# Which tile shape the products beside the weighings have, and a new list of pieces

## The chip, the cores and the metric

The kernel runs on one core of a Trainium2 chip. The metric is the device time of one execution in microseconds (us). Five engines work side by side, each through its own instructions in order: PE multiplies matrices (PEld is its loading of weights), DVE, ACT and POOL work element by element, SP issues most of the DMAs.

## The reference

What is computed, cut to what matters (S = 2048 rows, D = 512, 32 heads of width 16, 4 segments of L = 512 rows, F = 1792):

```
xn = layernorm(x)
q, k, v = xn @ wq, xn @ wk, xn @ wv           # split in heads and segments
for s in range(4):                            # M and z start at zero
    logits = q_s k_s^T * Dh**-0.5 + mask      # mask: -1e9 where the key lies after the query
    a_dot = softmax(logits) @ v_s
    a_mem = (phi(q_s) @ M) / (phi(q_s) @ z + 1e-6)
    o_s = g * a_mem + (1 - g) * a_dot         # g = sigmoid(beta), phi(t) = t + 1 if t > 0 else exp(t)
    M, z = M + phi(k_s)^T v_s, z + sum(phi(k_s))
out = x + o @ wo + silu(xn @ w1) @ w2
```

## The kernel before

The kernel is written as small pieces of work, and a list, ORDER, says in which order they are issued. Each word of the list is a piece's name followed by its numbers; the loop at L765 calls the functions of the table PIECES one after the other. Nothing is rearranged afterwards: every engine meets its own instructions in the order of the list, and semaphores make it wait for the others. So the list is the schedule of all engines at once.

The work is cut by segment s (512 rows), by block dt of 128 columns (8 heads) and by tile of 128 rows (t over all 16, or j within a segment). The pieces that matter here:

- S (scores, L634), 80 of them: a fifth of the scores of one block of one segment. Its matmuls use a quarter of PE's rows each (16 or 32 rows, four at a time), and write the four banks of psS, of which there is one buffer. ACT takes the exponential of all 2048 columns (L650) into one of seven buffers Pb, and POOL sets what lies behind the diagonal to zero (L658). A new line of the list begins at each S.
- E and O (weigh, L668), 16 each: the weights Pb times the values V, for the even and the odd heads of a block. Its matmuls use a quarter of PE's columns each (32 of 128), four at a time. Ev, Ea, Ov, Oa copy the result (oraw, odd), and SP moves the sums of the weights into zraw (L692) and the odd heads' rows into oraw (L711).
- k, q, v and h: products of the normed rows with wk, wq, wv and w1; a product of 512 columns is cut into parts (dense, L319, dense_mm, L309). ha is the tanh of h (L439), hv finishes silu into hT (L444); kv, qv, vv (and ka, qa, va on ACT) copy the others.
- o (out_mm, L577): one of the 18 products that add up to an output tile: 14 with w2 (from hT) and 4 with wo (from oT). oh is the same for one half of the last tile's columns. st and sh add x and store (L570, L614). In the last segment the tiles 2 and 3 are summed in psS.
- m, t, f and g pieces: the memory M and the maps phi; n (L548): phi(q) times M; s (L450): phi(q) times z, in column tiles of 32; r, w and, in the last segment, R, W: reciprocals of the sums and their weighting; z and d (spread, L518): DMAs that spread them over the rows, two for each; zv, dv, nv: the products and the sum that make oT (L536, L546, L557).
- xs, xq, xi, xg: statistics of the layernorm; Nv: its norm (L293); X, Xa, Xv and XD: its transposes; busy: matmuls of zeros.

The four banks that are not psS are shared by all other results of PE (bank, L298, four buffers). All matmuls but those of S, E, O and s are whole: 128 rows by 128 columns, one weight load each.

Of the kernel before, what the change touches and what calls it, by code (L numbers as in the profile page):

```python
# [15 lines left out]
ORDER = """  # L16
ones0 ones1 zeros xs0 xs1 xq0 xi0 busy44 xq1 Nv0 xi1 X0.1 Nv1 Xa0.1 busy6 X1.1 Xa1.1 v0.0.0 v0.0.1 xs2 xs3 xq2 v0.0.2 v0.0.3 xq3 xi2 va0.0 v0.1.0 v0.1.1 Nv2 v0.1.2 v0.1.3 va0.1 xi3 X2.1 Nv3 odd tb Xv2.1 k0.0.0 k0.0.1 X3.1 Xv3.1 k0.1.0 k0.2.0 k0.1.1 k0.0.2 k0.0.3 kv0.0 q0.0.0 q0.0.1 q0.0.2 q0.0.3 qa0.0 k0.1.2 xs7 fa0.0 k0.1.3 k0.2.1
S0 kv0.1 k0.3.0 k0.2.2 xs4 xs6 xs5 k0.3.1 q0.1.0 q0.1.1 q0.1.2 q0.1.3 xg4.4 k0.3.2 qa0.1 q0.3.0
S2 k0.3.3 v0.3.0 k0.2.3 kv0.2 q0.3.1 v0.3.1 q0.3.2 fp0.2 v0.3.2 q0.3.3 v0.3.3 fa0.2 kv0.3
S1 v0.2.0 h0.10.0 h0.10.1 qv0.3 h0.10.2 h0.11.0 v0.2.1 h0.10.3 Nv5 h0.11.1 h0.11.2 Nv6 ha0.10 fp0.0 vv0.3  # L20
S6 Nv7 hv0.10 q0.2.0 v0.2.2 q0.2.1 Nv4 v0.2.3 h0.11.3 XD5 h0.1.0 h0.1.1 ha0.11 XD7 h0.1.2
S5 q0.2.2 xs10 q0.2.3 vv0.2 h0.1.3 h0.5.0 h0.5.1 ha0.1 hv0.11 XD6 h0.13.0 qv0.2 h0.5.2 h0.5.3 h0.7.0
S3 ha0.5 h0.13.1 fv0.2 XD4 h0.7.1 xs13 h0.13.2 h0.13.3 hv0.1 xs9 h0.7.2 h0.7.3 ha0.13 E0 Ev0
S7 k1.1.0 t0.2 hv0.5 k1.1.1 ha0.7 k1.1.2 k1.1.3 xs11 q1.1.0 fp0.3 q1.1.1 q1.1.2 hv0.13 kv1.1 hv0.7 q1.1.3
S9 v1.1.0 xs8 qv1.1 v1.1.1 k1.0.0 lw0 xg8.4 k1.0.1 k1.0.2 E1 Ev1
S4 v1.3.0 k1.0.3 v1.1.2 fa0.3 kv1.0 v1.3.1 v1.3.2 v1.1.3 h0.4.0 h0.4.1 vv1.1 Nv10 h0.4.2
S10 k1.2.0 k1.2.1 k1.2.2 v1.3.3 h0.4.3 h0.2.0 h0.2.1 fv0.3 Nv8 vv1.3 ha0.4 k1.2.3 h0.2.2
S8 fp0.1 hv0.4 h0.2.3 O0 ha0.2 h0.8.0 h0.8.1 h0.8.2 Ov0
S14 q1.3.0 q1.3.1 tanh kv1.2 q1.3.2 h0.8.3 hv0.2 v1.2.0 Nv11 h1.11.0 v1.2.1 t0.3 ha0.8 h1.11.1 Nv9 xs12 q1.3.3
S11 hv0.8 XD10 v1.2.2 h1.11.2 h1.11.3 XD8 v1.2.3 XD9 O1 ha1.11  # L30
S12 qv1.3 vv1.2 k1.3.0 Ov1 h0.6.0 k1.3.1 k1.3.2 xs15 h0.6.1 fv0.0 h0.6.2 h0.6.3 q1.0.0 ha0.6 q1.0.1 hv1.11
S17 q1.0.2 k1.3.3 fa0.1 h0.0.0 h0.0.1 hv0.6 v1.0.0 xs14 h0.0.2 XD11 kv1.3 h0.0.3 q1.0.3
S16 m0.2 qv1.0 mv0.2 v1.0.1 E2 v1.0.2 h0.3.0 ha0.0 Ev2
S13 q1.2.0 h0.3.1 hv0.0 q1.2.1 xg12.4 h0.3.2 v1.0.3 h0.9.0 q1.2.2 h0.3.3 t0.0 ha0.3 vv1.0 h0.9.1
S15 h0.12.0 q1.2.3 h0.12.1 h0.12.2 fv0.1 h0.9.2 hv0.3 h0.9.3 h1.9.0 kind h1.9.1 ha0.9 h1.9.2 qv1.2 hv0.9
S18 fp1.0 h0.12.3 O2 E3 t0.1 h1.9.3 fp1.1 ha0.12 ha1.9
S19 Ev3 Ov2 hv1.9 k2.2.0 hv0.12 k2.2.1 fa1.0 kv2.2 h1.0.0 h1.0.1 h1.0.2 m0.0 h1.0.3
S21 Nv15 h1.8.0 mv0.0 v2.1.0 O3 ha1.0 h1.8.1 h1.8.2
S22 h1.8.3 Ov3 v2.1.1 hv1.0 ha1.8 vv2.1 v2.2.0 v2.2.1 o0.0.9 h1.10.0 Nv13
# [12 lines left out]
S38 v2.0.0 v2.0.1 q2.2.0 h1.6.3 XD14 ha1.6 q2.2.1 hv1.3
S33 h1.12.0 vv2.0 h1.13.0 fv1.3 hv1.6 qv2.2 h1.12.1 h1.13.1 h1.13.2 h1.13.3 gp1.2 ha1.13 E6 XD12
S34 h1.12.2 h1.12.3 ha1.12 hv1.13 v2.3.0 Ev6 v2.3.1 vv2.3 q2.0.0 o0.3.8
S37 o0.3.17 gv1.2 o0.3.16 fp2.0 q2.0.1 o0.3.3 q3.3.0 qv2.0 o0.3.4 ga1.3 t1.3 o0.3.13
S35 O6 hv1.12 q3.3.1 Ov6 k3.1.0 k3.1.1 fa2.0
S39 o0.3.9 kv3.1 gv1.3 h1.2.0 qv3.3 o0.3.14 h1.2.1 h1.2.2 fp2.3 h1.2.3 E7 ha1.2 fv2.0 fp2.1
S47 q3.1.0 o0.3.2 q3.1.1 ga2.2 Ev7 o0.3.10 O7
S41 qv3.1 o0.3.6 Ov7 m1.2 o0.3.5 o0.3.7 o0.3.15 mv1.2 fa2.1 m1.0 o0.3.11 hv1.2
S45 s1 q3.0.0 o0.3.12 fv2.1 gp2.2 mv1.0 sv1 r1.0 fa2.3 q3.0.1 v3.0.0  # L60
S42 h2.3.0 qv3.0 r1.1 v3.0.1 h2.3.1 ha2.3 vv3.0 t2.0 o0.3.0 o0.3.1 xl1.0 st0.3 h1.7.0
S44 h2.4.0 h2.4.1 r1.2 v3.3.0 r1.3 v3.3.1 ha2.4 w1 h1.7.1
S40 hv2.3 o1.0.3 vv3.3 o1.0.6 h1.7.2 hv2.4 o1.0.9 gv2.2 ga2.0 z1.2 fv2.3 v3.1.0 h1.7.3 v3.1.1
S46 ha1.7 vv3.1 v3.2.0 z1.1 d1.2 o1.0.1 v3.2.1 d1.1 o1.0.5 zv1.2 E8
S43 vv3.2 h2.8.0 hv1.7 d1.0 o1.0.11 h2.8.1 Ev8 k3.2.0 ha2.8 q3.2.0 dv1.2 d1.3
S49 q3.2.1 zv1.1 hv2.8 qv3.2 k3.2.1 gp2.0 z1.3 ka3.2 O8 xl2.0 E9 dv1.1
S48 o1.0.4 o1.0.2 k3.0.0 o1.0.13 Ev9 Ov8 n1.1 k3.0.1 o1.0.7 nv1.1 ka3.0
S51 n1.2 nv1.2 o1.0.10 dv1.3 h2.0.0 dv1.0 o1.0.12 zv1.3 xl1.2 o1.2.4 h2.0.1 ha2.0 o1.2.5
S50 o1.0.8 n1.3 o1.2.16 o1.2.10 hv2.0 o1.2.8 o1.0.15 O9 z1.0
S57 gv2.0 nv1.3 o1.2.13 h2.2.0 gp2.1 o1.0.17 o1.2.9 xl1.1 fp2.2 h2.2.1 ha2.2 Ov9 o1.1.12 o1.2.17  # L70
S52 o1.1.10 o1.2.0 o1.2.1 hv2.2 zv1.0 o1.1.4 o1.1.3 o1.2.3 o1.2.12 ga2.3 n1.0 o1.0.0 nv1.0 o1.1.8
S54 o1.2.11 o1.1.9 fa2.2 o1.1.5 o1.0.14 o1.1.16 o1.2.6 mw1.0 E10
S53 o1.0.16 o1.2.15 Ev10 o1.2.7 h2.7.0 h2.7.1 ha2.7 o1.2.2 o1.2.14
S59 fv2.2 st1.0 h2.1.0 st1.2 h2.1.1 o1.1.11 ha2.1 gp2.3 hv2.1 o1.1.14 o1.1.17 hv2.7 h2.11.0
S55 o1.1.2 o1.1.13 h2.11.1 o1.1.0 o1.1.1 o1.1.15 ha2.11 t2.3 o1.3.6 o1.1.6
S56 O10 gv2.3 o1.3.17 mw1.2 t2.1 o1.3.2 ga2.1 xl1.3 o1.1.7 o1.3.3 t2.2 Ov10 hv2.11 o1.3.5 o1.3.11 st1.1
S58 h2.6.0 h2.6.1 ha2.6 m2.0 E11 mv2.0
S63 h2.5.0 o1.3.16 h2.5.1 Ev11 o1.3.14 ha2.5 O11 hv2.6 Ov11
S60 h2.13.0 mw2.0 o1.3.0 hv2.5 gp3.1 h2.13.1 h2.10.0 ha2.13 gv2.1 o1.3.7 h2.10.1 ha2.10 o1.3.1 hv2.13
S61 s2 o1.3.9 o1.3.15 h3.1.0 hv2.10 o1.3.13 h3.1.1 xl2.3 o1.3.4 sv2 ha3.1 r2.3 r2.2 r2.0  # L80
S62 k3.3.0 r2.1 ga3.3 o1.3.8 w2 k3.3.1 d2.1 o1.3.12 d2.3 fill o1.3.10 gp3.3 st1.3 hv3.1 h2.9.0
S64 h2.9.1 m2.2 kv3.3 h3.3.0 h3.3.1 o2.3.2 z2.3 mv2.2 ha2.9
S66 ha3.3 E12 o2.3.3 o2.3.8 hv2.9 h3.0.0 Ev12 h3.0.1 ha3.0
S67 o2.3.11 z2.1 gv3.3 h2.12.0 o2.3.5 o2.3.10 h2.12.1 dv2.3 hv3.0 hv3.3 h3.4.0 o2.3.4 o2.0.6 ha2.12 z2.0 dv2.1
S65 zv2.3 o2.3.6 o2.3.0 h3.4.1 hv2.12 o2.0.12 o2.3.9 z2.2 o2.0.8 d2.0 o2.0.9 o2.3.13 zv2.1 n2.3 gp3.2 d2.2 ha3.4
S69 o2.0.5 xl2.1 hv3.4 o2.0.11 nv2.3 o2.3.1 o2.0.3 n2.1 nv2.1 ga3.2 o2.3.12 E13 Ev13
S68 O12 o2.0.1 o2.2.9 o2.3.15 zv2.0 dv2.0 o2.2.10 o2.2.0 Oa12 o2.2.12
# [14 lines left out]
def kernel(  # L102
# [474 lines left out]
    def out_mm(s, j, i, half=None):  # L577
# [21 lines left out]
        if s == LAST and j >= 2:  # L599
            for other, out in fin_out:  # L600
                if other != key:
                    tc.declare_no_dep(mm.ins, out.ins, reason="the outputs lie in banks of their own")
# [196 lines left out]
```

## Time and profile before

| | |
|---|---|
| median of 3 runs | 230.03 us (230.0 to 230.35) |
| the profiled execution | 231.8 us |
| its span, first to last instruction | 230.2 us |
| PE, ACT, DVE, POOL busy | 219.2, 199.3, 174.1, 113.3 us |
| exponentials (L650) | 80, 1.88 us each |
| instructions in the span | 5197 |

A row of the profile names the line of the kernel, the engine, the operation, what is written and read (out<-in), its shape and how often it ran; behind the bar stand the busy time and the mean of one in ns, then the idle time of the engine just before and what ended it. A timeline's row begins with the start and the length in us of one instruction, or of several merged (x4). For a matmul 16*128 or 32*128 are row tiles, 128*32 are column tiles and 128*128 is whole. Matmuls overlap: one of 512 columns shows as 0.38 us, and the next starts 0.216 us after it. "issue" stands for time in which an engine waited for nothing that the profile shows.

### The profile page before, as it was taken

How to read it: one execution, taken by the hardware profiler on the slowest of the kernel's cores; microseconds unless marked ns; L12 is line 12 of the kernel's file. 1: busy time of each engine (PE TensorE's matmuls, PEld its weight loads, DVE VectorE, ACT ScalarE, POOL GpSimd, SP SyncE). 2: the span in 40 equal slices, each digit the busy share in tenths (PEclk: the TensorE clock that was granted, in tenths of full speed). 3: DMA queues.
4: the chain of work that ended last, by engine and by line, in shares of the span. 5: the costliest groups of instructions: out<-in, count | busy, mean ns of one | idle time of the engine just before them, and what ended most of it. 6: DMA issues, size and time to landing. Idle time of an engine off the chain costs nothing.

```text
span 230.2 us, 5197 instructions
## 1 busy us (share of the span) xinstructions
PE 219.2 (95%) x1952; PEld 103.9 (45%) x1984; DVE 174.1 (76%) x348; ACT 199.3 (87%) x182; POOL 113.3 (49%) x173
## 2 busy tenths in 40 slices
PE   8999999999999999999999999999999999999993
PEld 8766544455434334343433433334343343435441
DVE  4789999997799587777698775585887765974833
ACT  3799999999999999999999999999999999893000
POOL 6049477656654576654944466353475355422000
PEclk9999999999999999999999999999999999999998
DMA  6993355132104532221023212161132211133122
GB/s 175 371 381 79 50 150 196 39 73 55 30 23 95 159 87 85 61 47 32 10 77 90 70 42 78 49 95 37 38 93 80 61 40 57 53 92 88 29 86 93
DMA packets 34777, 20.40 MB, mean 89 GB/s; under 512 B 15680, under 2 KB 34240, under 8 KB 34752
## 3 DMA queue, kind: packets, MB, share of 16 engines
q1 hardware_dynamic: 32128, 17.45, 27.4%
q10 hardware_dynamic: 2624, 2.62, 3.7%
q8 instruction: 15, 0.25, 0.5%
q14 instruction: 10, 0.08, 0.1%
HBM read 9.96 MB, written 2.10 MB: 52 GB/s over the span
## 4 chain that ended last, share of the span: by engine, by line
PE 69%; DVE 9%; ACT 8%; issue 5%; SPq 2%; POOL 2%; DMA 2%; DVEq 0%; ACTq 0%
PE ps L315 24%; PE psO L596 21%; PE psS L643 9%; PE psV L677 7%; ACT Pb L650 6%; PE ps L326 3%; ACT th L439 2%; PE psS L737 2%; DVE xn_t L293 2%; SPq L524 1%; PE psM L401 1%; DVE hT L444 1%; DVE stats L270 1%; POOL Pb L658 1%; DMA spr<-rz 1%
## 5 line engine op out<-in xcount | busy, mean ns | idle before, releaser
L650 ACT ACTIVATE Pb<-psS 128x2048 bf16<-128x2048 f32 x80 | 150.2, 1878 | 4.3 <-PE psS L643 3.2
L658 POOL TENSOR_SCALAR_AFFINE_SELECT Pb<-Pb 128x512 bf16<-128x512 bf16 (+1 forms) x112 | 80.5, 732 | 85.1 <-ACT Pb L650 84.9
L596 PE MATMUL psO<-w_sb,hT 128*128 128x512 bf16 x186 | 59.1, 381 | 0.8 <-issue 0.6
L444 DVE SCALAR_TENSOR_TENSOR hT<-th,ps 128x512 bf16<-128x512 bf16 x56 | 37.7, 681 | 16.1 <-ACT th L439 15.7
L315 PE MATMUL ps<-xnT,w_sb 128*128 128x512 bf16 x159 | 47.1, 380 | 0.8 <-issue 0.6
L596 PEld LDWEIGHTS <-hT 128*128 128x128 bf16 x238 | 21.8, 98 | 25.1 <-issue 6.2
L439 ACT ACTIVATE th<-ps 128x512 bf16<-128x512 f32 x56 | 32.7, 597 | 0.4 <-PE ps L315 0.4
L315 PEld LDWEIGHTS <-w_sb 128*128 128x128 bf16 x168 | 15.2, 98 | 18.3 <-issue 3.8
L677 PE MATMUL psV<-Pb,Vz 128*32 128x128 bf16 (+3 forms) x512 | 22.4, 302 | 0.5 <-DVE Vz L358 0.3
L596 PE MATMUL psO<-wo_sb,oT 128*128 128x512 bf16 x53 | 18.8, 380 | 0.3 <-issue 0.2
L643 PE MATMUL psS<-qT,kT 16*128 16x512 bf16 (+3 forms) x256 | 17.3, 302 | 0.9 <-ACT Pb L650 0.4
L315 PE MATMUL ps<-wv_sb,xnT 128*128 128x512 bf16 x60 | 18.1, 380 | 0.1
L643 PE MATMUL psS<-qT,kTo 32*128 32x512 bf16 (+3 forms) x256 | 17.2, 300 | 0.7 <-ACT Pb L650 0.4
L677 PEld LDWEIGHTS <-Vz 128*32 128x32 bf16 x512 | 11.0, 96 | 14.3 <-issue 4.6
L326 PE MATMUL ps<-xnT,w_sb 128*128 128x256 bf16 x112 | 16.4, 273 | 0.2 <-DVE z L414 0.2
L342 POOL TENSOR_SCALAR kTo<-kT,pm_odd 128x512 bf16<-128x512 bf16 x16 | 11.7, 736 | 8.5 <-DVE kT L341 7.6
L315 PE MATMUL ps<-xnT,wq_sb 128*128 128x512 bf16 x46 | 14.3, 381 | 0.0
L315 PE MATMUL ps<-xnT,wk_sb 128*128 128x512 bf16 x44 | 13.6, 380 | 0.7 <-DVE oraw L700 0.5
L707 DVE CAST odd<-psV 128x512 bf16<-128x512 f32 x14 | 9.6, 687 | 5.4 <-PE psV L677 5.3
L643 PEld LDWEIGHTS <-kT 16*128 16x128 bf16 x256 | 5.8, 92 | 17.1 <-issue 16.6
L326 PEld LDWEIGHTS <-w_sb 128*128 128x128 bf16 x112 | 10.5, 98 | 4.9 <-issue 1.5
L700 DVE CAST oraw<-psV 128x512 bf16<-128x512 f32 x15 | 10.3, 687 | 3.0 <-PE psV L677 2.8
(96 smaller groups left out, 262.9 us busy)
## 6 DMA issues: line engine op xcount, KB each, us to landing
spr<-rz SPq DMA_DIRECT2D x56, 64.0 KB
x_res<-in_A_x_dram SPq DMA_DIRECT2D x16, 128.0 KB
out_dram<-o_out SPq DMA_DIRECT2D x15, 128.0 KB
w_sb<-in_B_w_dram SPq DMA_DIRECT2D x1, 1792.0 KB
w_sb<-in_B_w_dram ACTq DMA_DIRECT2D x1, 1792.0 KB
x_hi<-in_A_x_dram SPq DMA_DIRECT2D x2, 512.0 KB
oraw<-odd SPq DMA_DIRECT2D x64, 16.0 KB
wv_sb<-in_A_wv_dram SPq DMA_DIRECT2D x2, 256.0 KB
```

The lines of the kernel that those rows point to most:

```text
L315: nc.tensor.matmul(sts[s][key][:, :], lhsT=lhsT(ki), rhs=rhs(ki), start=(ki == 0), stop=(ki == DT - 1))
L326: nc.tensor.matmul(sts[s][name, i][:, cols], lhsT=w_sb[:, ki, i * P : (i + 1) * P], rhs=xnT[:, ki, cols], start=(ki == 0), stop=(ki == DT ...
L342: nc.gpsimd.tensor_scalar(out=kTo[:, dt, :], in0=kT[:, dt, :], scalar1=pm_odd[:, 0:1], scalar2=1.0, op0=ALU.mult, op1=ALU.mult,)
L439: nc.scalar.activation(out=th[:], in_=sts[s]["h", ft][:, :], func=AF.Tanh, scale=0.5)
L444: nc.vector.scalar_tensor_tensor(out=st["hT"][:, ft, :], in0=st.pop(("th", ft))[:], scalar=1.0, in1=st.pop(("h", ft))[:, :], op0=ALU.add, ...
L596: mm = nc.tensor.matmul(st["psO", *key], lhsT=lhsT, rhs=rhs, start=len(done) == 1, stop=len(done) == FT + DT)
L643: nc.tensor.matmul(psS[:, g, c0 : c0 + nq], lhsT=kk[rows, dt, kt * P : (kt + 1) * P], rhs=st["qT"][rows, dt, kt * P : L], start=True, stop ...
L650: exp = nc.scalar.activation(out=Pb[:, :, :], in_=psS[:, :, :], func=AF.Exp, scale=SCALE)
L658: mask = nc.gpsimd.affine_select(out=blocks, in_=blocks, compare_op=ALU.is_ge, fill=0.0, base=0, pattern=[[0, blocks.shape[1]], [1, P]], c ...
L677: nc.tensor.matmul(psV[32 * g : 32 * g + 32, kt * P : L], lhsT=Vzs[s % 2][:, kt, 4 * dt + g, par : par + 2, :].rearrange("p a d -> p (a d) ...
L700: copy(out=oraw[:], in_=sts[s].pop(("psV", 0))[:, :])
L707: copy(out=odd[:], in_=sts[s].pop(("psV", 1))[:, :])
```

## The change

1. A helper, product, writes a whole product either as before or as four matmuls of 32 columns of the weights each, at the four column tiles. All products call it (dense_mm, dense, m_mm, n_mm, out_mm). A pass over the list sets which form each has: behind an S the products take the form of the next E, O or s if it comes ahead of the next S, and are whole otherwise; behind an E, O or s they stay column tiles up to the next S.
2. out_mm can make a part of the columns: oc is a half, od a quarter. 28 products o are made as two halves each and 14 as four quarters.
3. The statistics of a norm can be issued in two pieces, xc (sums) and xd (variance), and the list does so for the first tiles.
4. The list is new from its first line to its last.

```diff
+    narrow = [False]
+    def product(out, lhsT, rhs, start, stop):
+        if not narrow[0]:
+            return [nc.tensor.matmul(out, lhsT=lhsT, rhs=rhs, start=start, stop=stop, skip_group_check=True)]
+        return [
+            nc.tensor.matmul(
+                out[c : c + 32], lhsT=lhsT[:, c : c + 32], rhs=rhs, start=start, stop=stop,
+                tile_position=(0, c), skip_group_check=True,
+            )
+            for c in range(0, P, 32)
+        ]
...
-    def out_mm(s, j, i, half=None):
+    def out_mm(s, j, i, half=None, part=0, parts=1):
...
+        here = slice(part * width // parts, (part + 1) * width // parts)
+        cols = slice(first + here.start, first + here.stop)
...
-        mm = nc.tensor.matmul(
-            st["psO", *key], lhsT=lhsT, rhs=rhs, start=len(done) == 1, stop=len(done) == FT + DT
-        )
+        mms = product(st["psO", *key][:, here], lhsT, rhs, len(done) == 4, len(done) == 4 * (FT + DT))
...
-    for word in ORDER.split():
-        piece = word.rstrip("0123456789.")
+    words = ORDER.split()
+    pieces = [word.rstrip("0123456789.") for word in words]
+    TILED = {"S": "rows", "E": "cols", "O": "cols", "s": "cols", "X": "whole", "busy": "whole"}
+    ahead = ["rows"] * (len(words) + 1)
+    for i in reversed(range(len(words))):
+        ahead[i] = TILED.get(pieces[i], ahead[i + 1])
+    now = "whole"
+    for i, (word, piece) in enumerate(zip(words, pieces)):
+        if piece in TILED:
+            now = TILED[piece]
+        elif piece in ("k", "q", "v", "h", "m", "n", "o", "oc", "od", "oh"):
+            now = ahead[i] if now == "rows" else now
+            now = "whole" if now == "rows" else now
+        narrow[0] = now == "cols"
         PIECES[piece](*(int(n) for n in word[len(piece) :].split(".") if n))
```

The list before the first scores, one stretch from the middle of each, and its end from the last three S on, before (-) and after (+):

```diff
-ones0 ones1 zeros xs0 xs1 xq0 xi0 busy44 xq1 Nv0 xi1 X0.1 Nv1 Xa0.1 busy6 X1.1 Xa1.1 v0.0.0 v0.0.1 xs2 xs3 xq2 v0.0.2 v0.0.3 xq3 xi2 va0.0 v0.1.0 v0.1.1 Nv2 v0.1.2 v0.1.3 va0.1 xi3 X2.1 Nv3 odd tb Xv2.1 k0.0.0 k0.0.1 X3.1 Xv3.1 k0.1.0 k0.2.0 k0.1.1 k0.0.2 k0.0.3 kv0.0 q0.0.0 q0.0.1 q0.0.2 q0.0.3 qa0.0 k0.1.2 xs7 fa0.0 k0.1.3 k0.2.1
+ones0 ones1 zeros xc0 xd0 xc1 xq0 xi0 Nv0 busy44 xd1 xq1 xc2 xi1 X0.1 Nv1 xd2 Xa0.1 busy6 v0.0.0 v0.0.1 xq2 X1.1 Xa1.1 xs3 v0.0.2 v0.0.3 xq3 v0.1.0 xi2 v0.1.1 v0.1.2 v0.1.3 odd Nv2 xi3 X2.1 va0.0 k0.2.0 va0.1 Nv3 Xv2.1 X3.1 Xv3.1 k0.0.0 k0.0.1 k0.0.2 k0.0.3 q0.0.0 kv0.0 tb q0.0.1 q0.0.2 xs4 q0.0.3 qa0.0 k0.2.1 q0.3.0 fa0.0 q0.1.0
...
-S56 O10 gv2.3 o1.3.17 mw1.2 t2.1 o1.3.2 ga2.1 xl1.3 o1.1.7 o1.3.3 t2.2 Ov10 hv2.11 o1.3.5 o1.3.11 st1.1
+S58 Ov10 gp3.3 E11 oc1.3.1.0 gv2.1 m2.0 o1.3.13 Ev11 h2.6.1 ha2.6 o1.3.11 mv2.0
...
-S78 r3.2 o2.1.17 o2.1.1 o2.1.4 r3.1 o2.1.8 r3.3 h3.13.1 w3 o2.1.0 xl3.1 o2.1.2 R0.3 ha3.7 hv3.6 o2.1.9 R0.2 ha3.13 hv3.7 o2.1.16 hv3.13 R0.1
-S75 o2.1.5 h3.11.0 h3.11.1 ha3.11 R0.0 o3.1.8 d3.0 h3.9.0 h3.9.1 o2.1.14 W0 ha3.9 o2.1.7
-S76 o3.1.12 o2.1.11 d3.2 d3.1 o2.1.10 hv3.11 o2.1.13 dv3.2 o2.1.6 h3.10.0 dv3.0 z3.1 o2.1.15 h3.10.1 ha3.10 oh2.0 oh1.0 oh8.0 o3.2.4 o3.2.1 o3.1.4 hv3.9 oh3.1 oh5.1 z3.0 st2.1 O15 z3.2 hv3.10 E15 dv3.1 o3.0.5 o3.1.10 oh5.0 o3.2.0 o3.2.11 Ea15 Oa15 oh11.0 oh13.1 zv3.0 o3.0.12 n3.0 oh12.0 n3.2 o3.0.13 oh9.0 o3.1.0 o3.1.13 o3.2.5 oh13.0 zv3.1 nv3.0 oh10.0 zv3.2 nv3.2 o3.1.7 o3.0.0 o3.2.13 R1.0 oh6.0 oh0.0 xl3.0 R1.1 R1.2 o3.2.14 o3.2.16 o3.0.4 o3.2.9 R1.3 n3.1 o3.2.3 o3.2.12 oh3.0 d3.3 oh4.1 o3.1.11 o3.0.11 oh16.1 nv3.1 o3.0.7 o3.0.8 o3.1.16 o3.0.6 oh1.1 oh15.1 o3.0.10 oh7.1 oh0.1 o3.1.1 o3.2.6 o3.0.9 o3.2.8 o3.2.15 W1 o3.1.2 oh4.0 oh15.0 o3.1.3 o3.1.5 dv3.3 oh7.0 o3.0.15 o3.0.14 n3.3 z3.3 oh16.0 o3.0.1 o3.2.2 oh10.1 o3.2.7 xl3.2 zv3.3 o3.2.10 oh14.0 nv3.3 o3.0.3 oh14.1 o3.2.17 o3.0.17 st3.2 o3.0.2 oh11.1 o3.0.16 oh12.1 oh17.1 st3.0 oh17.0 oh6.1 oh9.1 sh0 oh8.1 oh2.1 o3.1.9 o3.1.14 sh1 o3.1.17 o3.1.6 o3.1.15 st3.1
+S76 o2.1.8 d3.0 d3.1 h3.9.1 o2.1.9 oc2.1.10.1 h3.13.0 ha3.9 od2.1.12.0 oc2.1.11.1 h3.13.1 xl3.3 hv3.9 o3.0.12 o2.1.16 ha3.13 o2.1.13
+S75 o3.0.5 hv3.13 o2.1.4 o3.0.4 R0.2 W0 o2.1.17 z3.0 h3.10.0 o3.1.8 h3.10.1 dv3.0 z3.2 ha3.10 od2.1.12.1 st2.1 o3.0.0 o3.1.6
+S78 o3.0.9 hv3.10 dv3.1 o3.1.1 h3.11.0 o3.0.8 h3.11.1 dv3.2 E15 oh13.1 oh4.1 ha3.11 z3.1 o3.2.13 Ea15 oh12.1 hv3.11 oh6.1 oh10.1 o3.2.1 O15 Oa15 oh11.1 oh2.1 oh12.0 o3.0.1 zv3.0 oh13.0 n3.1 od3.1.11.3 oh3.1 zv3.1 o3.2.0 oh10.0 n3.0 o3.1.2 nv3.0 o3.0.7 nv3.1 o3.1.12 oh9.1 oh8.0 o3.2.5 oh11.0 o3.1.7 o3.2.6 o3.0.13 oh8.1 R1.1 R1.0 o3.2.9 o3.1.14 d3.3 R1.3 o3.2.14 oc3.0.3.0 oh0.0 o3.0.6 o3.2.8 oc3.0.11.1 zv3.2 o3.1.10 n3.2 o3.2.10 oh9.0 R1.2 oh1.1 oh15.0 W1 nv3.2 oh15.1 o3.2.4 oc3.0.11.0 o3.1.5 o3.0.14 o3.2.11 oh1.0 o3.2.12 o3.2.2 oh6.0 o3.2.16 oh2.0 z3.3 oh7.0 oh0.1 dv3.3 oh3.0 od3.0.10.0 oh14.0 od3.1.11.1 oc3.1.0.0 o3.0.15 zv3.3 od3.1.11.0 oc3.0.3.1 n3.3 oc3.1.9.0 oh4.0 o3.2.3 xl3.0 o3.1.16 nv3.3 o3.2.15 od3.0.10.1 od3.0.10.2 o3.2.7 oh5.0 oh16.0 oh16.1 od3.0.10.3 oh14.1 o3.2.17 oh17.0 oh17.1 o3.0.2 o3.0.16 o3.0.17 od3.1.11.2 xl3.1 st3.2 oc3.1.9.1 oh7.1 oh5.1 sh0 o3.1.17 sh1 oc3.1.0.1 o3.1.3 o3.1.15 o3.1.13 st3.0 o3.1.4 st3.1
```

## The prediction

> **What bounds the kernel now.** I read the page's busy shares and its chain first, then the busy times by stage, then the timelines of ACT and PE, then PE's groups kept apart by shape, and last the end of the run.
>
> ```profile
> PE 219.2 (95%) x1952; PEld 103.9 (45%) x1984; DVE 174.1 (76%) x348; ACT 199.3 (87%) x182; POOL 113.3 (49%) x173
> PE 69%; DVE 9%; ACT 8%; issue 5%; SPq 2%; POOL 2%; DMA 2%; DVEq 0%; ACTq 0%
> ```
>
> PE is busy 95% of the span and carries 69% of the chain. The three stages (before the first exponential starts, from there to the start of the last one, the rest) show ACT beside it:
>
> ```profile
> 13.02:205.76 192.74, 187.50 (x1717) 83.65 (x1744) 153.27 (x300) 188.39 (x164) 107.96 (x155) 1.00 0.29 77
> 205.76:230.20 24.44, 19.86 (x131) 10.15 (x132) 12.79 (x26) 3.55 (x4) 1.22 (x2) 0.97 0.25 76
> ```
>
> (Stage, length, then busy PE, PEld, DVE, ACT, POOL.) For 192.74 us PE (187.50) and ACT (188.39) are both full; in the last 24.44 us ACT is done and PE works alone. ACT's timeline in the middle shows the beat:
>
> ```profile
> 126.15 1.88 ACT L650 ACTIVATE Pb<-psS 128x2048 bf16<-128x2048 f32 x1
> 127.92 0.59 ACT L439 ACTIVATE th<-ps 128x512 bf16<-128x512 f32 x1
> 128.53 1.88 ACT L650 ACTIVATE Pb<-psS 128x2048 bf16<-128x2048 f32 x1
> ```
>
> An exponential starts every 2.38 us: 1.88 of its own, and a small ACT piece while PE makes the next scores in the one buffer psS. Between two scores PE has 2.38 us to fill with products. PE's timeline shows what a change of array shape costs:
>
> ```profile
> 128.85 0.59 PE L315 MATMUL ps<-xnT,wk_sb 128*128 128x512 bf16 x2
> 129.38 1.27 PE L677 MATMUL psV<-Pb,Vz 128*32 128x512 bf16 x32
> 130.58 0.39 PE L643 MATMUL psS<-qT,kTo 32*128 32x512 bf16 x4
> ```
>
> Two whole products of 512 columns start 0.21 apart (0.59 less 0.38 of one), so the second starts at 129.06. The weighings (tiles 32 wide) follow at 129.38, 0.32 later: 0.10 more. They stream 2560 columns, four tiles at a time; at 0.216 per 512 that is 1.08, and the scores come after 1.20: again 0.10 and a little. A change of shape costs about 0.10 us.
>
> **The change, part by part.** *Shapes.* I counted them along both lists. Before, PE changes shape 194 times: 80 scores (row tiles), 32 weighings and 3 sums (column tiles), all else whole. After it, every product of a stretch between two scores that holds a weighing or a sum is written as four column tiles, so the stretch has one change at each end: 160 in all. 34 fewer at 0.10 is 3.4 us of PE. The columns streamed are the same (464,640); 56 halves and 56 quarters stand for 42 whole products, 70 pieces more at some 2.5 ns (a 128-column product takes 56 ns, four take 223 against 216): 0.2 us.
>
> *The price of a narrow product.* 367 products become 1468 matmuls with 1468 weight loads; PE's program grows from 3970 to 6312 instructions. The weighings are the same form:
>
> ```profile
> L677 PE MATMUL psV<-Pb,Vz 128*32 128x512 bf16 x128 | 12.8, 388 | 0.5 <-DVE Vz L358 0.3
> L677 PE MATMUL psV<-Pb,Vz 128*32 128x256 bf16 x128 | 9.1, 273 | 0.0
> L677 PE MATMUL psV<-Pb,Vz 128*32 128x128 bf16 x128 | 7.3, 219 | 0.0
> L401 PE MATMUL psM<-Vz,phiK 128*128 128x128 bf16 x48 | 3.7, 220 | 0.2 <-issue 0.2
> L596 PEld LDWEIGHTS <-hT 128*128 128x128 bf16 x238 | 21.8, 98 | 25.1 <-issue 6.2 <-DVE hT L444 0.3
> L677 PEld LDWEIGHTS <-Vz 128*32 128x32 bf16 x512 | 11.0, 96 | 14.3 <-issue 4.6 <-DVE hT L444 2.6 <-DVE oT L557 0.8
> ```
>
> One of 128 columns takes 219 ns narrow and 220 whole, and 32 matmuls in the 1.20 us above run at the pace of their columns. So I take 0 extra. From the other side: what the trace shows is short runs, at most 64 instructions in 1.20 us, 18.8 ns each; if lasting streams went no faster, eight would take 150 ns, which leaves 512-column products alone and adds 41 ns to a half and 94 to a quarter. In the other direction nothing is to be gained, since the columns are the same. The Trainium skill speaks against the change here: "TensorEngine Tiling (Array Packing)", in its restrictions, says that column tiling turns the fast weight load off. By that rule alone four loads in a row, at the row's 96 ns, would make a product 384 ns and the run some 82 us longer. The trace differs: 512 loads of 32 columns keep PEld busy for 11.0 us, 86 ns for four, so they overlap; I keep 0.
>
> *The stretches.* For each stretch I added its columns (0.216 per 512), its changes (0.10) and took the longest of PE's sum, the beat of 2.38, and 2.73 where ACT has two small pieces (the spacing of exponentials in such stretches). The 79 stretches give 192.57 before, against 192.74 in the trace. After, PE streams 2.75 us more in them (171.39 for 168.65) with 32 fewer changes, and the same sum gives 192.63: +0.06. So the middle doesn't get shorter: the freed time is filled with products taken from the end (2.1 us) and from ahead of the first scores (0.4).
>
> *The end.* PE's work after the last scores falls from 19.88 us to 17.54 (streaming 19.48 to 17.34; changes 4 to 2). Before, the last scores start at 205.31 and PE's last product at 226.14: 20.83, where the sum has 19.66, so 1.17 were waits. They belong to a chain through DMAs (chain of waits, then PE's timeline):
>
> ```profile
> 213.56 0.50 SPq L692
> 214.11 1.54 DMA zraw<-odd
> 215.67 1.78 DVE ri L507 x4
> ...
> 222.90 0.27 PE L596 MATMUL psS<-wo_sb,oT 128*128 128x256 bf16 x1
> 223.53 0.39 PE L596 MATMUL psS<-wo_sb,oT 128*128 128x512 bf16 x1 [0.36 <-DVE oT L557]
> 226.14 0.38 PE L596 MATMUL psO<-wo_sb,oT 128*128 128x512 bf16 x1
> ```
>
> The last odd sums are copied 5.6 us after the last scores, SP issues their DMAs at 8.25 behind others of 0.5 to 0.6 each, the reciprocals begin at 10.36, and the last oT is ready at 18.2, when PE was to use it at 17.1. In the new list the last scores are of a batch that only O15 needs: its copy comes at about 4.2, SP is free for it at 4.9, reciprocals can begin at 7.0 (the same 2.1 after the issue), DVE passes them in order with its sums until 10.0, the spreads land some 3 us after their issue (12.9), and the last oT is ready at 14.1; its first user stands at 14.9 in PE's sum. So the chain should no longer bind. I leave 0.4 of waits: O15 needs a bank that a copy frees at about 3.6 and stands at 3.45, and the first half product at 2.47 needs the buffer of the exponential that ends at 2.33. From the last scores to the last product: 17.33 + 0.4 = 17.73, against 20.83: 3.10 less. What follows (store, DMA, 4.06 us to the end of the span) stays.
>
> *The beginning.* The first norm moves ahead by the second tile's variance, but its transposes stay behind 44 matmuls of PE that end at 5.77; the second norm starts some 0.75 later behind the third tile's sums (0.69), and two products are moved ahead of its transposes to cover it. The second tile's products then start about 0.3 later, two k products fewer stand ahead of the q of the first scores (2 x 0.22), and q ends at about 11.7 as before (11.74). First scores: 0.05 earlier, give or take 0.3. If the cover fails, the second norm's delay costs up to 0.5.
>
> *Sum.* 230.2 - 0.05 + 0.06 - 3.10 = 227.1 against the profiled span of 230.2 (231.8 with what lies around it). The runs' median, 230.03, stands 0.17 under the span; less the same 3.1 it gives **227.0 us**.
>
> **The rivals.**
> - *Waits take part of it* (0.14): each stretch is filled to 2.36 or 2.37 of 2.38, so one late operand pushes all that follows. For it: 0.17 of such waits before and a wholly new order. Against it: DVE's load by stretch, added up the same way, never falls more than 2.3 us behind in the new list (3.0 in the old). 1.2 to 2.6 us lost: 228.2 to 229.6.
> - *The chain at the end stays as long* (0.06): if the last oT still comes 18.2 after the scores, 2.65 us of products follow it, and the end is at 20.8 as before: 230.1, no change. For it: SP's queue, where each DMA takes 0.5 to 0.7.
> - *The drain stays* (0.04): if narrow products after a weighing still cost 0.10, the new list has 219 changes; the same sum gives 196.2 for the stretches and 17.9 for the end: 231.0. Against: within the weighings the tiles change place with no gap.
> - *Matmuls pass at a fixed price each* (0.14, the slower side): at 150 ns for eight instructions the stretches grow by 6.7 and the end by 2.6: 236. The place is the end (102 narrow products, 44 of them halves, in a row) and the 30 narrow stretches, which have 0.01 to 0.4 of slack. It decides from some 13 ns per product on (the sum gives +3.1 there). For it: the trace of before averages 58 ns per PE instruction and shows nothing dense for longer than a weighing. Against: the tiles of a weighing start within 10 ns. "TensorE: Matmul & The Clock Gate" of the Trainium skill (part 1, on the 56 ns) gives a mode in which each matmul costs 62 ns of issue. Four would be 248 ns, and by the same sum the run 259; the 32 matmuls in 1.20 us, 37 ns each, speak against it, if not fully, since a full queue could hide it.
>
> **How the numbers follow.** Forecast 0.62, own range 226.0 to 228.2. With the first three rivals it reaches 231.0, and 0.14 above it and a little below 226.0 are left out: 226.0 to 231.0. Under 0.2% (0.46 us) a measurement of this kernel can't tell a difference. Faster: 0.62 + 0.14 = 0.76; same 0.06; slower 0.04 + 0.14 = 0.18.
>
> **What would show it.** Right: exponentials still 2.38 apart, 192.4 to 193 us from the first to the last; last scores near 205, last product some 17.7 after; narrow products of 512, 256 and 128 columns starting 216, 109 and 56 ns apart, and no gap of 0.3 between a product and a weighing. Wrong: narrow products further apart than their columns, idle PE with "issue" in the long narrow end, exponentials at 2.5 in narrow stretches, or PE waiting for oT (L557 before) at the end as now.

## The result, and the profile after

The changed kernel takes **229.07 us** (median of 6 runs, 228.36 to 229.25); beside it on the same chip the kernel before took 230.37 (230.00 to 231.45). The ratio is 0.9931, with a 95% interval of 0.991 to 0.9951: 1.3 to 1.6 us faster, where 3.0 were forecast. The profiled execution took 229.25 us and its span is 227.4, against a forecast of 227.1. So the forecast of the span was nearly met, and that of the time was not.

The page's busy shares and the engines of the chain, after:

```profile
PE 217.5 (96%) x3127; PEld 113.3 (50%) x3155; DVE 177.1 (78%) x350; ACT 198.5 (87%) x180; POOL 113.9 (50%) x173
PE 67%; ACT 17%; DVE 7%; issue 4%; POOL 2%; DMA 1%; DVEq 0%; SPq 0%; ACTq 0%
```

PE has 3127 rows of matmuls where it had 1952, since a narrow product (column tiles) is four of them, and is busy 1.7 us less. In the chain ACT now stands at 17% and SP's queue at 0%. The stages from the first exponential to the start of the last, and from there to the end (length, then busy PE, PEld, DVE, ACT, POOL):

```profile
12.89:205.93 193.04, 188.28 (x2586) 92.86 (x2615) 157.69 (x305) 187.69 (x162) 109.11 (x156) 1.00 0.29 78
205.93:227.40 21.47, 17.63 (x440) 11.04 (x432) 11.50 (x23) 3.43 (x4) 0.64 (x1) 1.00 0.27 79
```

The middle kept its length (192.74 before) with 0.8 us more of busy PE in it; the end fell from 24.44 to 21.47. The narrow products, apart by shape (busy time, mean ns of one):

```profile
L324 PE MATMUL psO<-w_sb,hT 128*32 128x512 bf16 x208 | 18.3, 380 | 0.0
L324 PE MATMUL psO<-w_sb,hT 128*32 128x128 bf16 x164 | 8.4, 219 | 0.0
L324 PE MATMUL psO<-w_sb,hT 128*32 128x256 bf16 x104 | 7.2, 273 | 0.0
L324 PEld LDWEIGHTS <-hT 128*32 128x32 bf16 x644 | 15.9, 97 | 9.3 <-issue 1.7
```

380, 219 and 273 ns are what whole products of 512, 128 and 256 columns show as well; 644 loads of 97 ns keep PEld busy for 15.9 us, 25 ns each, so about four overlap. PE's timeline behind the last scores shows the stretch that was to have no gap:

```profile
205.48 0.39 PE L662 MATMUL psS<-qT,kTo 32*128 32x512 bf16 x4
205.81 0.61 PE L324 MATMUL psO<-w_sb,hT 128*32 128x512 bf16 x8
206.25 0.60 PE L324 MATMUL ps<-xnT,w_sb 128*32 128x512 bf16 x8
206.68 0.39 PE L324 MATMUL psO<-w_sb,hT 128*32 128x512 bf16 x4
206.90 0.60 PE L324 MATMUL ps<-xnT,w_sb 128*32 128x512 bf16 x8
207.33 0.72 PE L696 MATMUL psV<-Pb,Vz 128*32 128x512 bf16 x16
207.87 1.15 PE L324 MATMUL psS<-w_sb,hT 128*32 128x256 bf16 x28
```

Products pass at 0.216 per 512 columns. The first weighing (L696 at 207.33) follows eight matmuls, two products, after 0.43, and is followed after 0.54, which is its own 1280 columns at that pace: no 0.10 at either side. The row at 207.87 merges five half products and two of 512 columns (2304 in all, 0.97); the second weighing, O15, starts at 209.07, 0.22 later than that, a wait of the kind for which the forecast left 0.4.

### The profile page after: what moved, and what is told of

Read it like the earlier page. It is cut to its first block, busy times and chain, and to the rows that moved or that the text cites. A ratio compares the mean times of both kernels' runs of the same rounds, so it can differ in the third digit from the quotient of the medians.

```text
span 227.4 us, 7551 instructions
## 1 busy us (share of the span) xinstructions
PE 217.5 (96%) x3127; PEld 113.3 (50%) x3155; DVE 177.1 (78%) x350; ACT 198.5 (87%) x180; POOL 113.9 (50%) x173
## 4 chain that ended last, share of the span: by engine, by line
PE 67%; ACT 17%; DVE 7%; issue 4%; POOL 2%; DMA 1%; DVEq 0%; SPq 0%; ACTq 0%
PE ps L322 20%; PE psO L322 13%; ACT Pb L669 12%; PE psO L324 8%; PE psS L662 8%; PE ps L324 6%; PE psV L696 5%; PE psS L324 3%; ACT th L457 3%; PE psS L756 2%; ACT ex L395 1%; DVE hT L462 1%; DVE kT L361 1%; DVE qT L371 1%; DVE xn_t L301 1%
## 5 line engine op out<-in xcount | busy, mean ns | idle before, releaser
L322 PE MATMUL ps<-xnT,w_sb 128*128 128x512 bf16 (+1 forms) x177 | 43.3, 340 | 0.8 <-issue 0.5
L322 PE MATMUL psO<-w_sb,hT 128*128 128x512 bf16 (+2 forms) x137 | 36.0, 339 | 0.7 <-issue 0.5
L324 PE MATMUL psO<-w_sb,hT 128*32 128x512 bf16 (+2 forms) x476 | 27.6, 301 | 0.0
L696 PE MATMUL psV<-Pb,Vz 128*32 128x128 bf16 (+3 forms) x512 | 23.1, 300 | 0.2
L324 PE MATMUL ps<-xnT,w_sb 128*32 128x512 bf16 (+1 forms) x384 | 21.8, 329 | 0.0
L324 PEld LDWEIGHTS <-hT 128*32 128x32 bf16 x644 | 15.9, 97 | 9.3 <-issue 1.7
L662 PE MATMUL psS<-qT,kT 16*128 16x128 bf16 (+3 forms) x256 | 17.3, 301 | 0.9 <-ACT Pb L669 0.8
L696 PEld LDWEIGHTS <-Vz 128*32 128x32 bf16 x512 | 13.1, 96 | 10.3 <-DVE hT L462 1.1
L662 PE MATMUL psS<-qT,kTo 32*128 32x384 bf16 (+3 forms) x256 | 17.2, 299 | 0.6 <-ACT Pb L669 0.2
L322 PE MATMUL ps<-xnT,wk_sb 128*128 128x512 bf16 (+1 forms) x66 | 15.4, 328 | 0.7 <-issue 0.5
L361 DVE CAST kT<-ps 128x512 bf16<-128x512 f32 x15 | 10.2, 689 | 4.9 <-PE ps L322 4.3
L322 PE MATMUL ps<-xnT,wq_sb 128*128 128x256 bf16 (+1 forms) x62 | 12.8, 324 | 0.4 <-issue 0.2
```

Source lines behind the costliest of these rows:

```text
L322: return [nc.tensor.matmul(out, lhsT=lhsT, rhs=rhs, start=start, stop=stop, skip_group_check=True)]
L324: nc.tensor.matmul(out[c : c + 32], lhsT=lhsT[:, c : c + 32], rhs=rhs, start=start, stop=stop, tile_position=(0, c), skip_group_check=True,)
L361: copy(out=kT[:, dt, :], in_=sts[s].pop(("k", dt))[:, :])
L662: nc.tensor.matmul(psS[:, g, c0 : c0 + nq], lhsT=kk[rows, dt, kt * P : (kt + 1) * P], rhs=st["qT"][rows, dt, kt * P : L], start=True, stop ...
L696: nc.tensor.matmul(psV[32 * g : 32 * g + 32, kt * P : L], lhsT=Vzs[s % 2][:, kt, 4 * dt + g, par : par + 2, :].rearrange("p a d -> p (a d) ...
```

## The experiments

Every profile here is of one execution. The table has its stages in us: start to first exponential, to the start of the last one, to the start of PE's last matmul, to the end of the span. In every run the time is the span and 1.6 to 1.8.

| kernel | head | middle | end of PE | rest | span |
|---|---|---|---|---|---|
| before | 13.02 | 192.74 | 20.38 | 4.01 | 230.15 |
| e1, before again | 12.59 | 192.77 | 20.34 | 3.85 | 229.54 |
| e7, e8, before | 12.57, 12.77 | 192.73, 192.77 | 20.11, 20.14 | 3.98, 3.93 | 229.40, 229.61 |
| e5, before, quarters | 13.00 | 193.65 | 19.16 | 4.04 | 229.85 |
| e10, before, shifted | 12.54 | 192.78 | 19.16 | 4.03 | 228.51 |
| e13, before, store on ACT | 13.19 | 192.73 | 19.38 | 3.75 | 229.05 |
| e3, e11, old list narrow | 13.08, 12.97 | 192.81, 193.16 | 19.10, 19.09 | 4.76, 4.87 | 229.74, 230.09 |
| e2, new list whole | 13.08 | 197.45 | 17.24 | 4.17 | 231.95 |
| e4, new list, end whole | 12.97 | 193.07 | 17.24 | 4.13 | 227.41 |
| after | 12.89 | 193.04 | 17.31 | 4.20 | 227.44 |
| e6, e12, after again | 12.85, 12.57 | 194.29, 194.29 | 17.18, 17.04 | 4.24, 4.16 | 228.56, 228.07 |
| e9, after, shifted | 12.84 | 193.07 | 17.55 | 4.19 | 227.65 |

### The parts of the change: e1 to e4

Theory A: the forecast's steps hold, and the profiled execution of before was slower than most. Rivals: the narrow form costs something per matmul, or the list alone does the work. The edits, each on one line of the pass over the list (e3 puts the old list under the new code):

```diff
 e2   narrow[0] = False
 e3   ORDER = the list before
 e4   narrow[0] = now == "cols" and i < words.index("S78")
```

> The kernel before, unchanged, profiled once more. Theory A (the profiled execution of before was a slow one: its 231.8 us stand 1.8 above the median of 230.03, and its last 20.83 us from the last scores to the last product hold 1.17 of waits behind DMAs, which differ from one execution to the next): runs of 230.0 to 230.5 with spans of about 228.5, and a profile of such a run in which the stretches take 192.6 to 192.9 us and the end 19.7 to 20.0. Theory B (the 1.7 us lie outside the span, or are the profiler's own): the spans of the runs are about 230 and the profile shows the end of 20.8 again.

Measured: 230.74 us, ratio 0.9993 (0.9972 to 1.0013). The profiled execution took 231.21, and its end is 20.34, again the long one: the short end that theory A expected in the profile did not come.

> The changed kernel with its new list, but every product whole: only the form of 367 products differs. Theory A (a narrow product costs nothing, a change of shape 0.10 us): PE changes shape 219 times instead of 160; by the sum of the prediction the stretches grow from 192.6 to 196.2 us and the end from 17.5 to 17.9, so 4.0 us more than the changed kernel: 233.0, ratio to before about 1.012. Theory B (narrow products cost some ns each, which the new list already pays): less than that, 231 to 232, as the 367 products are given back their price (5 ns each would be 1.0).

Measured: 233.62 us, ratio 1.0118 (1.009 to 1.0146). The same list with 219 shape changes instead of 160 has a middle of 197.45, 4.41 longer: 0.08 us for each of the 55 added changes that lie there. Its end is as short as after's.

> The old list with the new rule of forms: products beside weighings and sums as column tiles, 160 changes of shape instead of 194. Theory A (the gain needs the new list: the middle keeps the beat of 2.38 us, so freed PE time is only worth something in the stretches that were over the beat): the sum gives 192.3 instead of 192.6 for the stretches and 19.7 instead of 19.9 for the end, 0.5 us less than before in all: ratio 0.998. Theory B (the form itself carries the gain, 34 changes at 0.10): 3 us less, ratio 0.987. Theory C (narrow products cost time): slower than before.

Measured: 231.93 us, ratio 1.0042 (1.0025 to 1.006): slower by a us, a miss. The middle stays at 192.81 although 34 changes are gone. Most stretches keep ACT's beat; against before, others gain 0.38 in all, about what theory A expected, but the one at 74 us is 0.48 longer. There ACT issues the load of wo (L176) between two exponentials: 0.58 behind the end of the first (73.84), where before has 0.09, and the second exponential waits for it. What holds that issue up stays open. The "rest" is 0.75 longer; what the trace shows of that stands at e11.

> The changed kernel with the 102 products behind the last scores whole again; all else as changed. Theory A (a lasting run of narrow products goes at the pace of its columns): two more changes of shape, 0.2 us, and a first change put two times more around the weighings, 0.4 us more in all: 229.5. Theory B (in a lasting run eight instructions take longer than the 109 ns of a half product): less time than the changed kernel, by up to 2.5 us.

Measured: 229.09 us, ratio 0.9913 (0.9892 to 0.9935), as after's 0.9931. 102 products in a row cost the same narrow and whole. Equal times alone would leave a rival, since e4 adds four changes of shape, which were expected to cost 0.4 us. PE's rows settle it. Behind the last scores after loses 0.57 us against the pace of its columns, 0.48 of it in three waits (0.22 ahead of O15, 0.06, 0.20 for the last oT). e4 loses 0.51, 0.40 of it at its four changes (0.09 to 0.11 each). That leaves 0.09 and 0.11 over all 110 products and parts of a weighing: no price per narrow product.

So neither part gains by itself (list alone +2.9 us, form alone +1.2). Together they gain: the list alone shortens PE's end from 20.38 to 17.24 and lengthens the middle by 4.71, and the form takes 4.41 of that away.

### What shortened the end in one profile and not in the time: e5 to e8

e3's PE ended 1.2 to 1.3 us earlier than before's, where its sum has 0.2. SP's timeline shows why. Before (start, length in us of one issue or several):

```profile
202.31 6.74 SPq L524 DMA_DIRECT2D spr<-rz  x10
209.09 1.83 SPq L575 DMA_DIRECT2D out_dram<-o_out  x1
210.96 1.26 SPq L524 DMA_DIRECT2D spr<-rz  x2
212.32 1.14 SPq L692 DMA_DIRECT2D zraw<-oraw  x2
213.56 1.05 SPq L692 DMA_DIRECT2D zraw<-odd  x2
```

The store's issue takes 1.83 us, where the same line takes 0.3 to 0.6 elsewhere. SP issues without a pause here, so the last odd sums leave 1.3 later, and with them the reciprocals, the spreads and the last oT: the 1.17 us of waits in the prediction. Among the trace's DMA packets one of 16,384 bytes on queue 8 ("instruction" on the page) runs from 209.03 to 210.53. The page counts 15 such packets before and 24 after, one for some 260 of PE's instructions (3970 and 6312); e2, the new list whole, has 16. So these packets are taken here to be PE fetching its program, which is inferred from the counts:

```profile
q8 instruction: 15, 0.25, 0.5%
```

```profile
q8 instruction: 24, 0.39, 0.7%
```

e5 moves the fetch: 14 output products of the old list (segments 0 and 1) are cut into quarters, 84 more instructions on PE.

```diff
-o0.0.9 ...
+od0.0.9.0 od0.0.9.1 od0.0.9.2 od0.0.9.3 ...
```

> The old list with all products whole, except that 14 output products of segments 0 and 1 are cut into four quarters each: 84 more instructions on PE, 0.1 us more work, nothing else changed. It shifts PE's later program fetches some 5 us earlier, so that the one at 209.0 no longer falls on the store whose issue took SP 1.83 us instead of 0.46. Theory A (the fetch makes the store's issue long, which delays the last odd sums' way to oT, and PE waits 1.17 us at the end for that): the store's issue is back at about 0.5, the last oT comes about 1.2 us earlier (16.9 after the last scores, as in the old list with narrow products), the last product 19.7 after the last scores instead of 20.8, and the time is about 1.0 us under the kernel before: ratio 0.996. Rival B (the waits at the end have another cause, or are in the profiled executions alone): the same time or 0.1 us more, ratio 1.000. Rival C (the fetch now hits other issues of the same queue): a long issue elsewhere before the last scores, end as before, ratio 1.000.

Measured: 230.92 us, ratio 1.0022 (1.0008 to 1.0037), so not the gain of theory A. The store took 0.38, and PE's end 19.16: its mechanism, in the profile. But the middle grew by 0.9, nearly all in one step at 84 us (DVE's and PE's waits, 80 to 84 us):

```profile
DVE oT L554 <- DMA spr<-rz: 1.5, 1, 1.5
PEld L322 <- DVE oT L554: 0.9, 1, 0.9
```

Here a fetch runs from 78.43 to 79.31, while spreads issued from 75.5 on are landing; some of their 512-byte packets come only from 79.4 on, when it has ended, to 80.2 (before, they are there by 78.9, and the fetch begins at 79.3). oT is late, and PE, whose stretches are full, never makes it good. That the fetch held these packets up fits the times, but it is a single case.

> The changed kernel once more, beside the kernel before on the same chip. Theory A (the end gives 3.1 us where the kernel before loses 1.2 us to the long store issue, and the profiled execution of before was slower than most): 1.3 to 2.0 us under the kernel before, ratio 0.991 to 0.994, span near 227.4 in the profile. Rival (the gain is the full 3.1 and the first comparison was off): ratio 0.987.

Measured: 228.86 us, ratio 0.9929 (0.9912 to 0.9946). This profile's middle is 194.29, 1.25 over after's, again in steps: 1.01 at 138.8 and 0.20 at 146.2. SP ahead of that in after and in e6 (eight spreads, then a load of x):

```profile
121.78 5.19 SPq L542 DMA_DIRECT2D spr<-rz  x8
127.01 0.46 SPq L579 DMA_DIRECT2D x_res<-in_A_x_dram  x1
```

```profile
121.77 6.33 SPq L542 DMA_DIRECT2D spr<-rz  x8
128.15 0.47 SPq L579 DMA_DIRECT2D x_res<-in_A_x_dram  x1
```

In e6 one of the eight takes 1.74 instead of 0.60: it begins at 124.36, 0.08 behind a fetch at 124.28. In after the fetch begins at 124.36 together with the issue and does nothing to it. All behind it is 1.14 late, and in e6 DVE and ACT show:

```profile
135.92 0.65 DVE L554 TENSOR_TENSOR oT<-spr,oraw 128x512 bf16<-128x512 bf16 x1 [0.85 <-DMA spr<-rz]
138.82 1.88 ACT L669 ACTIVATE Pb<-psS 128x2048 bf16<-128x2048 f32 x1 [1.01 <-PE psS L662]
```

> The kernel before, one look for a further profile. Theory A: span between 228.4 and 230.2; the middle 192.7 to 192.8; the end 20.8 after the last scores whenever the store's issue takes 1.8 us, 19.7 where it takes 0.5; the head 12.6 to 13.1 by the time at which PE's clock turns full. Rival (the whole spread is in the head): the end always 20.8.

> The kernel before, one more look, expected as in the look ahead of it: span 228.4 to 230.2, middle 192.7 to 192.8, end 20.8 with a long store issue and 19.7 without it.

Measured: spans of 229.4 and 229.6, store issues of 1.59 and 1.62, PE's end 20.11 and 20.14. Four of four profiles of before have the long store, in executions of 231.07 to 231.8 us, while medians of its runs lie between 230.03 and 230.74. So the profiled executions are slower than the medians beside them by 0.5 to 1.8.

### Shifting the fetch: e9 to e12

In e9 and e10 PE's first 44 matmuls become 22 of twice the columns, 44 instructions fewer; nothing later is touched.

```diff
-... busy44 ...
+... busy22 ...
-nc.tensor.matmul(idle[:, 0:P], lhsT=zraw[:, 0:P], rhs=zraw[:, 0:P], ...)
+cols = 2 * P if n == 22 else P
+nc.tensor.matmul(idle[:, 0:cols], lhsT=zraw[:, 0:P], rhs=zraw[:, 0:cols], ...)
```

> The changed kernel, with the 44 matmuls of 128 columns that PE runs at the very start replaced by 22 of 256 columns: the same columns, 44 instructions fewer on PE, so that every later program fetch of PE comes some 44 instructions (0.8 to 3 us) later, and nothing else is changed. Theory A (a fetch of 16 KB holds up a DMA issue of SP that begins just behind it, or packets behind it on one of the 16 DMA engines, and in the full stretches such a delay of a spread makes PE late): the end as before (17.2 from the last exponential to the last matmul); the middle between 193.0 and 194.5, and what it has over 193.0 in jumps of 0.2 to 1.2 us at single stretches, each behind a fetch, at other places than in the profile with 194.29 (137.8 and 145.0). The time may go either way by 1 us: ratio to the kernel before 0.987 to 0.996. Rival B (the jump at 137.8 belongs to the list, not to the fetch): a jump at the same place or none, ratio 0.993.

Measured: 229.02 us, ratio 0.9945 (0.9921 to 0.9969). The middle is 193.07 with no step over 0.06 against after. One spread's issue takes 1.19 here (125.10, 0.10 behind a fetch), and no step follows it.

> The kernel before with the same 22 matmuls of 256 columns at the start: the fetch at 209.0 comes some 0.8 us later, at 209.9, behind the store's issue at 209.1 or 208.6. Theory A: the store's issue takes 0.5 again, the end from the last exponential to the last matmul is 19.2 instead of 20.1 to 20.4, unless the later fetch hits one of the four issues behind the store as hard; the middle 192.7 unless another fetch now delays a spread (as with the quarters, where it took 0.8). Ratio 0.996, or 0.999 to 1.002 where a new delay takes it back. Rival B (the store's issue is long by itself): 1.6 to 1.8 us as before, the end 20.2, ratio 1.000.

Measured: in the profile just what theory A says. SP in e10, the fetch now at 210.70:

```profile
201.87 6.74 SPq L524 DMA_DIRECT2D spr<-rz  x10
208.65 0.46 SPq L575 DMA_DIRECT2D out_dram<-o_out  x1
209.15 1.27 SPq L524 DMA_DIRECT2D spr<-rz  x2
```

PE's end 19.16 and a span of 228.51, 0.9 to 1.6 under the four profiles of before. Of before's 230.15 its span lacks 1.64: 1.22 in PE's end and 0.48 in the head. But the median is 230.52, ratio 1.0004 (0.9984 to 1.0024): in the time nothing was gained, where theory A had 0.996.

> The old list with the narrow form once more, one look for a second profile. Its 12 timed runs were 230.93 to 232.68, above what its one profile (span 229.74, middle 192.81) explains. Theory A (22 program fetches instead of 15 delay spreads in some executions): a middle of 193 to 194.5 with jumps at single stretches behind a fetch. Rival B (narrow products cost a little everywhere): no jumps, and the 1 us spread over many stretches or in the end.

Measured: span 230.09; one step of 0.38 against e3 in the middle, at 74 us, and a "rest" of 4.87. The step is e3's own stretch again: the load of wo is issued at 74.08, 0.96 behind the exponential, and the fetch there begins later, at 74.34. So theory A's steps behind a fetch are not what came. The last stores of e11, then of e10:

```profile
223.77 1.74 SPq L591 DMA_DIRECT2D out_dram<-o_out  x2
225.63 0.85 SPq L637 DMA_DIRECT2D out_dram<-o_half  x2
226.90 0.33 SPq L591 DMA_DIRECT2D out_dram<-o_out  x1
```

```profile
223.01 1.10 SPq L575 DMA_DIRECT2D out_dram<-o_out  x2
224.24 0.85 SPq L618 DMA_DIRECT2D out_dram<-o_half  x2
225.62 0.33 SPq L575 DMA_DIRECT2D out_dram<-o_out  x1
```

With the narrow form the old list has a fetch at 224.19 (223.36 in e3) among the last stores, and two of them take 1.74 (1.44) for 1.10. But the last store also leaves 0.56 (0.28) behind DVE's last sum, 0.03 in e10, and the span ends 3.19 (3.36) behind that store's issue, 2.6 to 2.9 in before's list whole. The fetch is over by 225.14 (224.60), so it is not shown to do all of this, and the rest stays open. The spans of 229.74 and 230.09 agree with the median of 231.93 less 1.7 to 0.5 and 0.1.

> The changed kernel, one look for a third profile. Theory A: head 12.6 to 13.1, end 17.2 and 4.2; the middle 193.0 or, with a delayed spread, up to 194.3, in jumps. Rival B: the middle 193.0 always.

Measured: middle 194.29 again, the same steps at 138.6 and 145.9, and the same cause: a spread's issue of 1.78 at 124.09, just behind a fetch at 124.03. This execution took 229.78 us; of the 25 runs of after and its shifted form, five are at 229.6 or more, e6's profiled one (230.3) among them.

### Whether the timed runs have the wait: e13

```diff
-nc.sync.dma_start(out=out_flat[t * P : (t + 1) * P, :], in_=o_out[:])
+queue = nc.scalar if (s, j) == (2, 1) else nc.sync
+queue.dma_start(out=out_flat[t * P : (t + 1) * P, :], in_=o_out[:])
```

> The kernel before, with the one store that took SP 1.6 to 1.8 us (output tile 1 of segment 2) issued on ACT's queue, so that SP goes on to the last odd sums without it, whatever PE fetches. Five of five profiles of the unchanged list have the long issue, but shifting the fetch, which took 1.0 us from the end in the profile, left the median time where it was. Theory A (the timed executions as a rule don't have the long issue, so the profiled ones were some 0.8 us slower than most): the profile's end from the last exponential to the last matmul 19.2 as with the shift, span near 228.6; the median time as before, ratio 0.999 to 1.001. Rival B (most executions have it, and the shift's gain was eaten by other delays): about 1.0 us less, ratio 0.996.

Measured: 230.37 us beside 230.67, ratio 0.9989 (0.9975 to 1.0004). (Profiles of the unchanged list with the long store are four, not five.) In e13's profile the fetch (209.02) hits the next spread, 1.31 at 209.25, so that the gain on SP is smaller than planned; still PE's end is 19.38, 0.7 to 1.0 under before. In the time 0 to 0.6 us are gained, and 1.0 lies outside the interval. The head of this profile is long (13.19), since PE waits 0.46 there for the load of wk.

## Why the forecast had the sign and the span, and missed the time

**The failed step is the last of the sum:** "The runs' median, 230.03, stands 0.17 under the span; less the same 3.1 it gives 227.0 us". Its 3.10 for the end counts the 1.17 us of waits that the profile of before showed. They came from one store's issue of 1.83 us. The prediction read that queue as issues "of 0.5 to 0.6 each" and passed over this one. With the long issue gone, PE's end in the profile is 1.0 to 1.2 us shorter (e10, e13), and the median stays nearly as it was. So the wait belonged to the profiled execution, and most timed runs, as far as these two show, did not have it. The step also set a time beside a span: 230.03 is a whole time, and such a run's span is near 228.4. The profiled execution took 231.8, 1.8 us over the median, and that surplus had to sit in some rows of the trace; e10 shows 1.22 of it in the end and 0.48 in the head.

Made against e10's profile, which lacks the long store, the sum closes: middle +0.26 (193.04 for 192.78), end -1.85 (17.31 for 19.16), rest +0.17, together -1.42. The head is left out of it, as no difference can be told there. The two comparisons gave 1.30 (229.07 for 230.37) and 1.68 (228.86 for 230.54).

The other steps:

- *Head, -0.05:* no difference can be told. It varies from 12.57 to 13.19 in the four profiles of before and e13's. In the four it goes with PE's granted clock, which turned full at 4.3, 5.6, 6.4 and 7.0 us (heads 12.57, 12.59, 12.77, 13.02); the 13.19 has the wait for wk.
- *Middle, +0.06:* right in kind, 0.24 short. The sum by stretches (192.63) misses by 0.41; 0.28 of it lie in one stretch, the fourth (2.66 for 2.38), whose scores wait for POOL's kTo, and the others cancel. That narrow products cost nothing and save the changes held. Two of three profiles of after have 1.25 more, from the fetch, which the sum knew nothing of; most timed runs are too fast to have it (after's fastest took 228.36).
- *End of PE:* from last scores to last product 17.75, forecast 17.73, in part by luck. The forecast's 0.4 of waits stood for O15 and the first half product; 0.22 came at O15 and none at the half product. The last oT came at 15.2 and not at 14.1, since here too one issue was long, 1.68 us at 213.50 behind a fetch at 213.33, and PE waited 0.20 for it at 220.6.
- *"What follows stays":* 0.2 longer. Two output tiles now end together, and DVE and SP pass them one after the other (DVE's and SP's last rows):

```profile
223.15 1.28 DVE L586 SCALAR_TENSOR_TENSOR o_out<-psO,x_res 128x512 bf16<-128x512 f32 x2
```

```profile
224.18 0.81 SPq L591 DMA_DIRECT2D out_dram<-o_out  x2
```

- *The rivals:* "matmuls pass at a fixed price" fell with the rows behind the last scores, after's and e4's; "the drain stays" with the timeline above and e2, which shows what it would have cost; "the chain at the end stays as long" with 17.75. "Waits take part of it" names a loss that two profiles have, by a cause that it did not name.

The prediction weighed a rule of the Trainium skill: by "TensorEngine Tiling (Array Packing)", restrictions, column tiling turns the fast weight load off. Its estimate of what that would cost, some 82 us, did not come: PEld is busy 25 ns per load of 32 columns. Whether these loads are the fast ones no trace here shows.

**Open:** why the profiled executions of before meet the long store and most timed ones do not. No trace of an execution of the unchanged kernel without it exists; that most lack it is inferred from e10, e13, the sum, and the times: of 98 timed runs of before on record 18 reach 231.07, the fastest profiled execution. e10 too has three of 12 there, so the long store is not the only thing that makes a run slow, and how much of e10's missing gain other delays took back was not separated. The lists of times hold a hint: the profiled execution is the first listed of its series, and in the four long lists of before's times the first is 231.51, 231.58, 230.98 and 232.67, over their medians of 230.39 to 230.70.

## What to carry to other kernels

A wait that is to be counted as gain must be in the median run, not only in the profiled one: where the profiled execution is slower than the median by more than the effect, look for the rows that hold the surplus before taking it off the median. Freeing an engine gained only with work from a stage that it alone bounds moved into the freed time; the form or the list alone lost. Many small instructions can have a price beside their own time: 24 program fetches for 15 here, each of which can meet a DMA issue, and 1.25 us in two of three profiles.

## What the runs showed of the hardware

- PE's program comes in packets of 16 KB (one for some 260 instructions; that they are PE's is inferred from the counts), 0.9 to 1.7 us each.
- A DMA issue of SP that begins close to the start of one can take 1.2 to 1.8 us instead of 0.4 to 0.6: 1.83, 1.82, 1.59, 1.62 for before's store, 1.74 and 1.78 for the spread of e6 and e12, 1.68 for after's L730. Not each does, and it goes by the kind of DMA. Of all issues in the 15 traces that begin from 0.2 ahead of a packet's start to 0.3 behind it, over 1 us took 40 of 50 that move odd rows (`oraw<-odd`; 4 of 847 that begin over 0.6 from one), 4 of 18 stores, 5 of 34 spreads and none of 55 that move sums (`zraw`).
- Packets of a spread came some 1.3 us late in e5 (80.2 for 78.9), while such a packet was under way; a single case.
- Where the fetches fall can be shifted by 44 instructions at the very start of PE's program: the one at 209.03 of before is at 210.70 in e10.
- A change between array shapes costs 0.09 to 0.11 us in single places (before's middle, e4's end), and 0.08 net over the 55 that e2 adds to the middle.
- Narrow products of 512, 256 and 128 columns start 0.216, 0.109 and 0.055 us apart in a row of over a hundred (after, behind the last scores), like whole ones.
